# Which weight chunks are streamed in a recurrent attention kernel, and where the last tokens' output projection runs

## The chip, the cores and the metric

One core of one Trainium2 chip. The metric is the device time of one execution in microseconds (us), lower is better.

## The reference

The program computes two independent things and joins them: a long convolution (part A, the first 0.3 ms, not touched by the change) and attention over 64 segments of 32 tokens with 8 memory tokens (part B). The output at the memory tokens of one segment is the memory of the next, so part B is a chain of 64 segments. Cut to part B:

```python
# D = 1024, 32 heads of 128; seg_len 32, M = 8 memory tokens, n_seg = 64
for s in range(n_seg):
    h = concat([mem, x[:, s*32:(s+1)*32]], axis=1)          # 40 rows
    q, k, v = h @ Wq, h @ Wk, h @ Wv                        # three 1024 x 4096 weights, bf16
    p = softmax(mask(q @ k.T * scale))
    o = (p @ v) @ Wo                                        # 4096 x 1024
    mem = o[:, :M]                                          # needed by the next segment
    outs.append(o[:, M:])
```

The four weights are 32 MB; the kernel keeps part of them on the chip and reads the rest again in every segment.

## The kernel before

The weights are cut into 64 chunks of 512 KB: 8 each for K, Q, V in two head groups (48), and 16 for Wo. 43 chunks stay resident (`Wearly`, `Wlate`); 21 are streamed in every segment through a ring of six buffers, chosen evenly over the 64:

```python
NSTREAM = 21; RING = 6
order = [...K0, Q0, K1, Q1, V0, V1 (8 chunks each), then Wo (16)...]
for i in range(64):
    if ((i + 1) * NSTREAM) // 64 > (i * NSTREAM) // 64:
        streamed.add(order[i])
# [cut]
def fetch():                       # next chunk of the endless list of streamed chunks
    t = ring.tile([128, 2048], BF, tag="wring", name="wring")
    nc.sync.dma_start(t[:], stream_src(uses[n]))
def done(ch):                      # a streamed chunk was used: its buffer is refilled
    if ch in streamed:
        used[0] += 1
        fetch()
```

The last eight of a segment's 32 input tokens are called last tokens; their output does not feed the recurrence, so it can wait. Their attention output is gathered in `OTB` over four consecutive segments, and every fourth segment (`j == NB - 1`, below "the fourth") multiplies each Wo chunk twice: once for its own other 32 rows (24 tokens and the 8 memory rows), and once for the 32 rows of `OTB`. The four matmuls that use one chunk in a projection are called a group below: the "last V group" is the end of a segment's projections. That four column groups work side by side shows in the timeline of the kernel before: four matmuls of 256 columns, of 0.28 us each, start 0.107 us after the four before them.

```python
def load_x(s):                     # 192 KB: input rows and ready-made K/Q parts of segment s
    rec = one.tile([128, 768], BF, tag="rec", name="rec")     # one buffer
    nc.gpsimd.dma_start(rec[:], REC[:, s, :])
# [cut] fill_mem: PE transposes Y, VectorE copies the memory rows into rec (line 614)

def out_proj(hps, OT):
    for hp in hps:
        w = weight((3, hp, 0))
        for hh in range(2):
            lhs = [(OT[:, c, i, :], 0)]
            if j == NB - 1:
                lhs.append((OTB[:, c, 4 * g + i, :], 256))
            for src, o in lhs:
                for dq in range(4):          # four column groups of the array, side by side
                    nc.tensor.matmul(yacc[32 * dq:32 * dq + 32, o:o + 256], lhsT=src,
                                     rhs=w[:, hh * 1024 + dq * 256:hh * 1024 + (dq + 1) * 256], ...)
        done(ch)

# one segment, cut to its order on PE
k0 = Proj(0, 0).run().evac(); q0 = Proj(1, 0).run().evac()    # Proj: 8 chunks, 4 matmuls each
k1 = ...; q1 = ...; scores(0); pv0 = Proj(2, 0)...; scores(1)
pv1 = Proj(2, 1).run(4); attend(0); pv1.run(4)
if s + 1 < n_seg:
    load_x(s + 1)                  # waits until the last V matmul has read rec
out_proj(range(0, 5), OT0); attend(1); out_proj(range(5, 8), OT0); out_proj(range(8, 16), OT1)
nc.scalar.copy(Y[:], yacc[:, 0:256])
fill_mem(pend[s + 1][0], Y)        # then the next segment's K projection can start
```

Of the kernel before, what the change touches and what calls it, by code (L numbers as in the profile page):

```python
# [9 lines left out]
BF = mybir.dt.bfloat16  # L10
F32 = mybir.dt.float32
# [10 lines left out]
NSTREAM = 21  # L22
# [370 lines left out]
def b_kernel(ctx: ExitStack, tc, x, mem0, Wq, Wk, Wv, Wo, outb, n_seg):  # L393
    nc = tc.nc
    SEG = 32
    NX = 24
    NB = 4
# [14 lines left out]
    for hp in range(16):  # L412
        order.append((3, hp, 0))
    streamed = set()
    for i in range(64):
        if ((i + 1) * NSTREAM) // 64 > (i * NSTREAM) // 64:
            streamed.add(order[i])
    resident = [ch for ch in order if ch not in streamed]
    early = resident[:NEARLY]
# [3 lines left out]
    ring_order = [ch for ch in order if ch in streamed]  # L423

    def dram_chunk(ch):
        m, a, g = ch
        return Wo_v[a] if m == 3 else W_v[m][a, g]

    def dst_view(ap, ch):
        return ap.rearrange("p (hh d) -> p hh d", hh=2) if ch[0] == 3 else ap  # L430

    def stream_src(ch):
        return WS[ring_order.index(ch), :, 0:2048]
# [3 lines left out]
    REC = dram.tile([128, n_seg, 768], BF, name="REC")  # L437
    VBD = dram.tile([n_seg, 8, 4, 4, 256], BF, name="VBD")
    WS = dram.tile([len(ring_order), 128, PITCH], BF, name="WS")
    for ch in ring_order:  # L440
        if ch[0] == 3:
            nc.gpsimd.dma_start(dst_view(stream_src(ch), ch), dram_chunk(ch))

    const = ctx.enter_context(tc.tile_pool(name="b_const", bufs=1))
    ident = const.tile([128, 128], BF, name="ident")
    make_identity(nc, ident[:])
# [4 lines left out]
    res = {}  # L451
# [38 lines left out]
    with ExitStack() as c0:  # L490
# [42 lines left out]
        for m in (0, 1):  # L533
            for g in range(2):
                ws = group(m, g)
                stage = st.tile([128, n_seg, 16, 8], BF, tag="stage", name="stage")
                for hl in range(16):
                    ps = ps0.tile([128, 512], F32, tag="ps0", name="kb_ps")
                    for kc in range(8):
                        nc.tensor.matmul(ps[:], lhsT=ws[kc][:, hl * 128:(hl + 1) * 128],  # L540
                                         rhs=XBT[:, kc].rearrange("p s t -> p (s t)"),
                                         start=(kc == 0), stop=(kc == 7))
                    evac(stage[:, :, hl, :], ps[:].rearrange("p (s t) -> p s t", t=8))
                o = 256 * (m + 1) + 128 * g
                nc.sync.dma_start(REC[:, :, o:o + 128], stage[:].rearrange("p s h t -> p s (h t)"))
        for g in range(2):
            ws = group(2, g)
            for tb in range(4):
                vst = st.tile([128, 4, 512], BF, tag="vst", name="vst")
                for c in range(4):  # L550
                    ps = ps0.tile([128, 512], F32, tag="ps0", name="vb_ps")
                    for kc in range(8):
                        nc.tensor.matmul(ps[:], lhsT=XBT[:, kc, 16 * tb:16 * tb + 16, :].rearrange("p s t -> p (s t)"),  # L553
                                         rhs=ws[kc][:, c * 512:(c + 1) * 512], start=(kc == 0), stop=(kc == 7))
# [13 lines left out]
    one = ctx.enter_context(tc.tile_pool(name="b_one", bufs=1))  # L568
    two = ctx.enter_context(tc.tile_pool(name="b_two", bufs=2))
    ps_acc = ctx.enter_context(tc.tile_pool(name="b_ps_acc", bufs=2, space=PSUM))  # L570
# [8 lines left out]
    def fetch():  # L579
        n = len(loaded)  # L580
        if n < len(uses):
            t = ring.tile([128, 2048], BF, tag="wring", name="wring")
            nc.sync.dma_start(t[:], stream_src(uses[n]))
            loaded.append(t)

    def weight(ch):
        if ch in res:
            return res[ch]
        assert uses[used[0]] == ch
        return loaded[used[0]]  # L590

    def done(ch):
        if ch in streamed:
            loaded[used[0]] = None
            used[0] += 1
            fetch()
# [21 lines left out]
    with tc.manual_schedule():  # L618
# [6 lines left out]
            nc.scalar.dma_start(Y0[32 * dq + NX:32 * dq + SEG, :], mem0[:, dq * 256:(dq + 1) * 256])  # L625
        fill_mem(pend[0][0], Y0)

        OTB = None
        for s in range(n_seg):
            b, j = s // NB, s % NB  # L630
            hT, KBs, QBs = pend.pop(s)
# [16 lines left out]
            class Proj:  # L648


                def __init__(self, m, g):
                    self.m, self.g, self.kc = m, g, 0
                    self.acc = ps_acc.tile([128, 512], F32, tag="acc", name="acc")

                def run(self, n=8):
                    for kc in range(self.kc, self.kc + n):
                        ch = (self.m, kc, self.g)
                        w = weight(ch)
                        for c in range(4):
                            nc.tensor.matmul(self.acc[32 * c:32 * c + 32, :], lhsT=hT[:, kc, :],  # L660
                                             rhs=w[:, c * 512:(c + 1) * 512],
                                             start=(kc == 0), stop=(kc == 7), tile_position=(0, 32 * c))
                        done(ch)
                    self.kc += n
                    return self
# [30 lines left out]
            def softmax_b(S):  # L696
                ssum = two.tile([128, 5], F32, tag="ssum", name="ssum")
                nc.vector.tensor_reduce(out=ssum[:], in_=S, op=ALU.add, axis=AX.X)
                nc.vector.reciprocal(ssum[:], ssum[:])
                nc.vector.tensor_tensor(out=P_pad[:, :, 0:32], in0=S[:, :, 0:32],  # L700
                                        in1=ssum[:].unsqueeze(2).to_broadcast([128, 5, 32]), op=ALU.mult)
                own = P_pad[:].rearrange("p b k -> p (b k)")[:, 32:320].rearrange("p (i w) -> p i w", w=72)
                nc.vector.tensor_tensor(out=own[:, 0:4, 0:8], in0=S[:, 0:4, 32:40],
                                        in1=ssum[:, 0:4].unsqueeze(2).to_broadcast([128, 4, 8]), op=ALU.mult)
                nc.vector.scalar_tensor_tensor(
                    out=P_pad[:, 4, 32:64].rearrange("p (i t) -> p i t", i=4),
                    in0=S[:, 4:5, 32:40].to_broadcast([128, 4, 8]), scalar=ssum[:, 4:5],
                    in1=rowhead[:].unsqueeze(2).to_broadcast([128, 4, 8]), op0=ALU.mult, op1=ALU.mult)
                PT = one.tile([128, 2, 4, 40], BF, tag="PT", name="PT")
                for kb in range(2):  # L710
                    ks = slice(32 * kb, 32 * kb + 32)
                    nc.vector.transpose(out=PT[:, kb, :, 0:32], in_=P_pad[:, 0:4, ks])
                    nc.vector.transpose(out=PT[:, kb, :, 32:40], in_=P_pad[:, 4, ks])
                return PT
# [14 lines left out]
            def o_view(g):  # L729
                return OTp[:, :, 160 * g:160 * g + 160].rearrange("p c (i q) -> p c i q", i=4)  # L730

            def evac_o(g):
                OT = one.tile([128, 4, 4, 32], BF, tag="rotA" if g else "rotB", name="OT")
                nc.scalar.copy(OT[:], o_view(g)[:, :, :, 0:32])  # L734
                return OT

            def evac_ob(g):
                nc.vector.tensor_copy(OTB[:, :, 4 * g:4 * g + 4, 8 * j:8 * j + 8], o_view(g)[:, :, :, 32:40])  # L738

            def out_proj(hps, OT):  # L740
                for hp in hps:
                    ch = (3, hp, 0)
                    w = weight(ch)
                    for hh in range(2):
                        h = 2 * hp + hh
                        g, c, i = h // 16, (h % 16) // 4, h % 4
                        lhs = [(OT[:, c, i, :], 0)]
                        if j == NB - 1:
                            lhs.append((OTB[:, c, 4 * g + i, :], 256))
                        for src, o in lhs:  # L750
                            for dq in range(4):
                                nc.tensor.matmul(yacc[32 * dq:32 * dq + 32, o:o + 256], lhsT=src,  # L752
                                                 rhs=w[:, hh * 1024 + dq * 256:hh * 1024 + (dq + 1) * 256],
                                                 start=(h == 0 and o == 0), stop=(h == 31 and o == 0),
                                                 skip_group_check=(o > 0), tile_position=(0, 32 * dq))
                    done(ch)

            if j == 0:
                OTB = one.tile([128, 4, 8, 32], BF, tag="OTB", name="OTB")
            Sp = ps_s.tile([128, 2, 5, 40], F32, tag="S", name="S")  # L760
            OTp = ps_o.tile([128, 4, 512], F32, tag="OTp", name="OTp")
            k0 = Proj(0, 0).run().evac()
            q0 = Proj(1, 0).run().evac()
            KT0 = keys(0)
            last_queries(0)
# [19 lines left out]
            pv1 = Proj(2, 1).run(4)  # L785
            attend(0, PT0, V0, OTp)
            OT0 = evac_o(0)
            PT1 = softmax_b(Sp[:, 1])
            evac_ob(0)
            pv1.run(4)  # L790
# [3 lines left out]
            yacc = ps_acc.tile([128, 512], F32, tag="acc", name="yacc")  # L794
            out_proj(range(0, 5), OT0)
            attend(1, PT1, V1, OTp)
            OT1 = evac_o(1)
            evac_ob(1)
            out_proj(range(5, 8), OT0)
            out_proj(range(8, 16), OT1)  # L800
            Y = one.tile([128, 256], BF, tag="Y", name="Y")
            nc.scalar.copy(Y[:], yacc[:, 0:256])  # L802
            if s + 1 < n_seg:
                fill_mem(pend[s + 1][0], Y)
            nc.gpsimd.dma_start(bass.AP(outb.tensor, outb.offset + SEG * s * 2048, [[256, 4], [2048, 32], [1, 256]]), Y[:])  # L805
            if j == NB - 1:
                YB = one.tile([128, 256], BF, tag="OTB", name="YB")
                nc.vector.tensor_copy(YB[:], yacc[:, 256:512])
                for dq in range(4):
                    nc.gpsimd.dma_start(  # L810
                        bass.AP(outb.tensor, outb.offset + (SEG * NB * b + NX) * 2048 + 256 * dq,
                                [[2048 * SEG, NB], [2048, 8], [1, 256]]), YB[32 * dq:32 * dq + 32, :])


@with_exitstack
# [65 lines left out]
```

## Time and profile before

| | us |
|---|---|
| median of the first three runs | 2481.6 (2478.2 to 2485.7) |
| span of the profiled execution | 2487.5 |
| part A, preparation and start of B, up to the first segment's Y | 602.7 |
| ordinary segment (three of four) | 28.6 |
| the fourth segment | 33.1 |

Starts of the ScalarE copies of `Y`, each of which ends a segment (timeline of ScalarE, kernel before; start, duration, instruction, idle time before it):

```profile
1367.89 0.37 ACT L802 CAST Y<-yacc 128x256 bf16<-128x256 f32 x1 [3.33 <-PE yacc L752]
...
1400.97 0.37 ACT L802 CAST Y<-yacc 128x256 bf16<-128x256 f32 x1 [6.61 <-PE yacc L752]
...
1429.90 0.37 ACT L802 CAST Y<-yacc 128x256 bf16<-128x256 f32 x1 [4.55 <-PE yacc L752]
...
1457.74 0.37 ACT L802 CAST Y<-yacc 128x256 bf16<-128x256 f32 x1 [3.88 <-PE yacc L752]
```

The first difference, 33.1 us, is a fourth segment, the next two, 28.9 and 27.8, are ordinary ones. Windows of the kernel before, over the end of that fourth segment and then of an ordinary one:

```profile
core 0: us, PE busy (x) PEld busy (x) DVE busy (x) ACT busy (x) POOL busy (x), PEclk, DMA share, GB/s
...
1392.00:1396.00 4.00, 2.70 (x117) 2.62 (x120) 0.29 (x1) 0.58 (x1) 0.00 (x0) 1.00 1.04 399
1396.00:1400.00 4.00, 1.88 (x71) 1.60 (x63) 0.00 (x0) 0.00 (x0) 0.00 (x0) 1.00 0.84 308
1400.00:1404.00 4.00, 3.20 (x75) 1.77 (x70) 0.53 (x2) 0.37 (x1) 0.72 (x1) 1.00 0.70 225
1404.00:1408.00 4.00, 3.18 (x56) 1.38 (x49) 0.42 (x1) 1.17 (x2) 0.01 (x1) 1.00 0.94 284
...
1424.00:1428.00 4.00, 2.62 (x100) 1.70 (x92) 0.29 (x1) 0.58 (x1) 0.00 (x0) 1.00 1.03 400
1428.00:1432.00 4.00, 2.75 (x54) 1.43 (x57) 0.19 (x1) 0.37 (x1) 1.44 (x3) 1.00 1.03 411
```

The last column is the point: around the Y of the ordinary segment (1429.90) the DMA engines never slow down; around the Y of the fourth (1400.97) they fall to 225 GB/s for want of requests (between 1388.14 and 1400.96 the ring's issues lie 1.3 to 3.7 us apart, and a chunk takes 1.28 us).

The chain of waits before that same Y (start, length, what; "issue" is time in which PE waited for nothing that the profile shows):

```profile
1391.84 1.46 issue
...
1396.58 2.12 issue
```

The output projection of this fourth segment stood still twice, and not for the ring. (The prediction's 1.6 and 2.4 us are the same two stops, counted from the start of one matmul to the start of the next.) Such stops are called fetch waits below, after the queue that the page calls "instruction": they end 1.2 to 1.6 us after one of its packets has ended.

### The profile page before, as it was taken

Reading aid. Unit: us, or ns where it says so; the run is one execution under the profiler, and the core shown is the slowest. Engines: PE = TensorE matmul, PEld = TensorE weight load, DVE = VectorE, ACT = ScalarE, POOL = GpSimd, SP = SyncE. Lnnn points to the kernel's source line nnn. Section 1 sums busy time; section 2 is a strip of 40 time slices with the busy share of each in tenths; the row PEclk is TensorE's granted clock in tenths of the full one; section 3 lists DMA queues with packets and bytes.
Section 4 is the critical chain, followed back from the end, with each engine's and each line's share of the span. In section 5 each row is a group of like instructions: output and inputs, shape, how many; then the busy total and the mean of one; then the engine's idle time right before and its main releaser. Section 6 shows DMA issues by size and latency. Waiting matters only on the chain.

```text
span 2487.5 us, 76464 instructions
## 1 busy us (share of the span) xinstructions
PE 1782.3 (72%) x33598; PEld 886.9 (36%) x33620; DVE 674.8 (27%) x2203; ACT 639.9 (26%) x1143; POOL 365.5 (15%) x1019
## 2 busy tenths in 40 slices
PE   3555279845777777777777777777777777777776
PEld 1221044322343333433343334343434343343433
DVE  5977222111222222222222222222222222222222
ACT  6965011101222222222222222222222222222221
POOL 5034000000111101111111111111111111111011
PEclk8888679878999999999999999999999999999999
DMA  8886965579999999999999999999999999999997
GB/s 286 309 280 216 361 225 143 174 249 393 399 374 393 387 379 396 373 400 376 401 377 398 372 399 360 394 368 402 360 398 374 400 366 400 368 386 385 373 389 288
DMA packets 317559, 875.09 MB, mean 352 GB/s; under 512 B 84684, under 2 KB 92908, under 8 KB 317223
## 3 DMA queue, kind: packets, MB, share of 16 engines
q1 hardware_dynamic: 287064, 800.75, 84.7%
q0 software_dynamic: 20048, 45.76, 5.3%
q10 hardware_dynamic: 10112, 23.68, 2.8%
q8 instruction: 263, 4.31, 0.7%
q14 instruction: 72, 0.59, 0.1%
HBM read 810.69 MB, written 62.39 MB: 351 GB/s over the span
## 4 chain that ended last, share of the span: by engine, by line
DMA 53%; PE 31%; issue 5%; DVE 3%; POOL 1%; ACT 1%; SPq 0%; DVEq 0%; POOLq 0%; ACTq 0%
DMA wring<-WS 47%; PE acc L660 12%; PE yacc L752 7%; PE kb_ps L540 4%; PE vb_ps L553 2%; PE qk_tp L675 1%; DMA pw<-in_B_Wv_dram 1%; DMA Wearly<-in_B_Wk_dram 1%; DMA zt<-SZ 1%; POOL Yre L342 1%; DMA Wlate<-in_B_Wv_dram 1%; DMA X_sb<-in_B_x_dram 1%; PE S L683 1%; PE S L679 1%; ACT Y L802 0%
## 5 line engine op out<-in xcount | busy, mean ns | idle before, releaser
L660 PEld LDWEIGHTS <-rec 128*32 128x32 bf16 x12288 | 326.7, 98 | 640.2 <-issue 422.0
L660 PE MATMUL acc<-wring,rec 128*32 128x512 bf16 x3840 | 394.8, 398 | 201.1 <-DMA wring<-WS 190.7
L669 ACT CAST qkv_sb<-acc 128x512 bf16<-128x512 f32 x384 | 224.7, 585 | 843.3 <-PE acc L660 796.5
L660 PE MATMUL acc<-Wearly,rec 128*32 128x512 bf16 x4608 | 378.1, 404 | 21.6 <-DVE rec L614 21.6
L660 PE MATMUL acc<-Wlate,rec 128*32 128x512 bf16 x3840 | 331.7, 386 | 0.2 <-issue 0.2
L752 PEld LDWEIGHTS <-OT 128*32 128x32 bf16 x8192 | 239.3, 99 | 247.9 <-issue 183.3
L752 PE MATMUL yacc<-Wlate,OT 128*32 128x256 bf16 x5120 | 261.4, 283 | 30.2 <-issue 29.8
L752 PE MATMUL yacc<-wring,OT 128*32 128x256 bf16 x3072 | 183.9, 284 | 127.9 <-DMA wring<-WS 111.6
L637 POOL COPY KT<-rec 128x128 bf16<-128x128 bf16 x128 | 38.7, 302 | 657.1 <-PE S L686 591.3
L805 POOL DMA_DIRECT2D out_dram<-Y x64 | 46.2, 721 | 565.1 <-ACT Y L802 556.2
L766 DVE COPY KT<-qk_tp 128x512 bf16<-128x512 bf16 x64 | 27.2, 425 | 359.2 <-PE qk_tp L675 359.2
L614 DVE COPY rec<-y_tp 128x64 bf16<-128x64 bf16 x64 | 12.3, 192 | 405.4 <-PE y_tp L613 405.4
L734 ACT CAST OT<-OTp 128x512 bf16<-128x512 f32 x128 | 74.9, 585 | 183.6 <-PE OTp L725 179.9
L691 DVE TENSOR_REDUCE mx<-S 128x5 f32<-128x200 f32 x128 | 47.2, 368 | 244.1 <-PE S L686 238.2
L802 ACT CAST Y<-yacc 128x256 bf16<-128x256 f32 x64 | 23.8, 372 | 340.6 <-PE yacc L752 340.6
L675 PE MATMUL qk_tp<-ident,qkv_sb 128*128 128x128 bf16 x1024 | 102.8, 224 | 0.0
L752 PE MATMUL yacc<-Wlate,OTB 128*32 128x256 bf16 x1280 | 91.1, 291 | 15.7 <-issue 15.7
L607 POOL DMA_DIRECT2D rec<-REC x64 | 37.0, 578 | 403.9 <-issue 272.6
L752 PEld LDWEIGHTS <-OTB 128*32 128x32 bf16 x2048 | 82.0, 103 | 29.1 <-issue 23.0
L738 DVE CAST OTB<-OTp 128x128 bf16<-128x128 f32 x128 | 34.7, 271 | 206.9 <-ACT OT L734 206.9
L675 PEld LDWEIGHTS <-qkv_sb 128*128 128x128 bf16 x1024 | 58.5, 98 | 77.1 <-issue 62.8
L540 PE MATMUL kb_ps<-XBT,Wearly 128*128 128x512 bf16 x281 | 83.0, 384 | 1.7 <-ACT XBT L507 1.2
(197 smaller groups left out, 2163.6 us busy)
## 6 DMA issues: line engine op xcount, KB each, us to landing
wring<-WS SPq DMA_DIRECT2D x1344, 512.0 KB, 7.5
rec<-REC POOLq DMA_DIRECT2D x64, 192.0 KB, 6.3
SK<-s_sb SPq DMA_DIRECT2D x16, 512.0 KB, 4.6
SU<-s_sb SPq DMA_DIRECT2D x16, 512.0 KB, 3.4
Kg<-SK ACTq DMA_DIRECT2D x32, 256.0 KB, 5.0
Ug<-SU SPq DMA_DIRECT2D x32, 256.0 KB, 5.1
REC<-stage SPq DMA_DIRECT2D x4, 2048.0 KB, 13.2
pw<-in_B_Wv_dram SPq DMA_DIRECT2D x16, 512.0 KB, 8.2
```

The source lines that it names most:

```text
L540: nc.tensor.matmul(ps[:], lhsT=ws[kc][:, hl * 128:(hl + 1) * 128], rhs=XBT[:, kc].rearrange("p s t -> p (s t)"), start=(kc == 0), stop=(kc ...
L553: nc.tensor.matmul(ps[:], lhsT=XBT[:, kc, 16 * tb:16 * tb + 16, :].rearrange("p s t -> p (s t)"), rhs=ws[kc][:, c * 512:(c + 1) * 512], st ...
L607: nc.gpsimd.dma_start(rec[:], REC[:, s, :])
L637: nc.gpsimd.tensor_copy(KT[:, :, :, 32:40], KBs[:, 128 * g:128 * g + 128].rearrange("p (c i t) -> p i c t", c=4, i=4))
L660: nc.tensor.matmul(self.acc[32 * c:32 * c + 32, :], lhsT=hT[:, kc, :], rhs=w[:, c * 512:(c + 1) * 512], start=(kc == 0), stop=(kc == 7), t ...
L669: nc.scalar.copy(sb[:], self.acc[:])
L675: nc.tensor.transpose(tp[:, i * 128:(i + 1) * 128], sb[:, i * 128:(i + 1) * 128], ident[:])
L691: nc.vector.tensor_reduce(out=mx[:], in_=S, op=ALU.max, axis=AX.X)
L734: nc.scalar.copy(OT[:], o_view(g)[:, :, :, 0:32])
L738: nc.vector.tensor_copy(OTB[:, :, 4 * g:4 * g + 4, 8 * j:8 * j + 8], o_view(g)[:, :, :, 32:40])
L752: nc.tensor.matmul(yacc[32 * dq:32 * dq + 32, o:o + 256], lhsT=src, rhs=w[:, hh * 1024 + dq * 256:hh * 1024 + (dq + 1) * 256], start=(h == ...
L805: nc.gpsimd.dma_start(bass.AP(outb.tensor, outb.offset + SEG * s * 2048, [[256, 4], [2048, 32], [1, 256]]), Y[:])
```

## The change

Its intent: keep every Wo chunk resident, so that the output projection never waits for the ring, and take the doubled work out of the fourth output projection: it runs in a `Tail` after Y and between the first eight K chunks of the next segment. Sizes, number of streamed chunks and ring stay the same. The core of the diff, cuts marked:

```diff
-    for i in range(64):
-        if ((i + 1) * NSTREAM) // 64 > (i * NSTREAM) // 64:
+    for i in range(48):
+        if ((i + 1) * NSTREAM) // 48 > (i * NSTREAM) // 48:
             streamed.add(order[i])
# [cut] the copies of streamed Wo chunks to WS fall away
+        class Tail:
+            def __init__(self, OTB, b):
+                self.OTB, self.b, self.h = OTB, b, 0
+                self.acc = ps_acc.tile([128, 512], F32, tag="acc", name="tail_acc")
+            def run(self, n):       # the next n heads: 4 matmuls each, resident weights
# [cut]
# [cut] out_proj loses the OTB part and done(ch)
-            k0 = Proj(0, 0).run().evac()
+            k0 = Proj(0, 0)
+            for _ in range(8):
+                k0.run(1)
+                if tail is not None:
+                    tail.run(3)
+            k0 = k0.evac()
# [cut]
             nc.scalar.copy(Y[:], yacc[:, 0:256])
+            if j == NB - 1:
+                tail = Tail(OTB, b)
+                tail.run(6)
             if s + 1 < n_seg:
                 fill_mem(pend[s + 1][0], Y)
# [cut] output DMA
+            if tail is not None:
+                tail.run(4 if s + 1 < n_seg else 32)
```

More of the change, by code (lines that the diff above doesn't have):

```diff
@@ L439, in b_kernel @@
     WS = dram.tile([len(ring_order), 128, PITCH], BF, name="WS")
-    for ch in ring_order:
-        if ch[0] == 3:
-            nc.gpsimd.dma_start(dst_view(stream_src(ch), ch), dram_chunk(ch))
     const = ctx.enter_context(tc.tile_pool(name="b_const", bufs=1))
@@ L626, in b_kernel, with store @@
         fill_mem(pend[0][0], Y0)
-        OTB = None
+        class Tail:
[3 more added lines that the diff above has]
+            def run(self, n):
+                for h in range(self.h, min(self.h + n, 32)):
+                    w = res[(3, h // 2, 0)]
+                    g, c, i = h // 16, (h % 16) // 4, h % 4
+                    for dq in range(4):
+                        o = (h % 2) * 1024 + dq * 256
+                        nc.tensor.matmul(self.acc[32 * dq:32 * dq + 32, 0:256], lhsT=self.OTB[:, c, 4 * g + i, :],
+                                         rhs=w[:, o:o + 256], start=(h == 0), stop=(h == 31),
+                                         tile_position=(0, 32 * dq))
+                    if h == 31:
+                        self.store()
+                self.h = min(self.h + n, 32)
+            def store(self):
+                YB = one.tile([128, 256], BF, tag="OTB", name="YB")
+                nc.vector.tensor_copy(YB[:], self.acc[:, 0:256])
+                for dq in range(4):
+                    nc.gpsimd.dma_start(
+                        bass.AP(outb.tensor, outb.offset + (SEG * NB * self.b + NX) * 2048 + 256 * dq,
+                                [[2048 * SEG, NB], [2048, 8], [1, 256]]), YB[32 * dq:32 * dq + 32, :])
+        OTB = tail = None
         for s in range(n_seg):
@@ L746, in out_proj @@
                         g, c, i = h // 16, (h % 16) // 4, h % 4
-                        lhs = [(OT[:, c, i, :], 0)]
-                        if j == NB - 1:
-                            lhs.append((OTB[:, c, 4 * g + i, :], 256))
-                        for src, o in lhs:
-                            for dq in range(4):
-                                nc.tensor.matmul(yacc[32 * dq:32 * dq + 32, o:o + 256], lhsT=src,
-                                                 rhs=w[:, hh * 1024 + dq * 256:hh * 1024 + (dq + 1) * 256],
-                                                 start=(h == 0 and o == 0), stop=(h == 31 and o == 0),
-                                                 skip_group_check=(o > 0), tile_position=(0, 32 * dq))
-                    done(ch)
-            if j == 0:
-                OTB = one.tile([128, 4, 8, 32], BF, tag="OTB", name="OTB")
+                        for dq in range(4):
+                            nc.tensor.matmul(yacc[32 * dq:32 * dq + 32, 0:256], lhsT=OT[:, c, i, :],
+                                             rhs=w[:, hh * 1024 + dq * 256:hh * 1024 + (dq + 1) * 256],
+                                             start=(h == 0), stop=(h == 31), tile_position=(0, 32 * dq))
             Sp = ps_s.tile([128, 2, 5, 40], F32, tag="S", name="S")
             OTp = ps_o.tile([128, 4, 512], F32, tag="OTp", name="OTp")
-            k0 = Proj(0, 0).run().evac()
+            k0 = Proj(0, 0)
[4 more added lines that the diff above has]
+            k0 = k0.evac()
+            tail = None
             q0 = Proj(1, 0).run().evac()
@@ L787, in b_kernel @@
             OT0 = evac_o(0)
+            if j == 0:
+                OTB = one.tile([128, 4, 8, 32], BF, tag="OTB", name="OTB")
             PT1 = softmax_b(Sp[:, 1])
@@ L805, in b_kernel @@
             nc.gpsimd.dma_start(bass.AP(outb.tensor, outb.offset + SEG * s * 2048, [[256, 4], [2048, 32], [1, 256]]), Y[:])
-            if j == NB - 1:
-                YB = one.tile([128, 256], BF, tag="OTB", name="YB")
-                nc.vector.tensor_copy(YB[:], yacc[:, 256:512])
-                for dq in range(4):
-                    nc.gpsimd.dma_start(
-                        bass.AP(outb.tensor, outb.offset + (SEG * NB * b + NX) * 2048 + 256 * dq,
-                                [[2048 * SEG, NB], [2048, 8], [1, 256]]), YB[32 * dq:32 * dq + 32, :])
+            if tail is not None:
+                tail.run(4 if s + 1 < n_seg else 32)
 @with_exitstack
```

## The prediction

> **What bounds the kernel now.** The first 574 us build the convolution and tables; then 64 segments run back to back. Between the ScalarE copies that end a segment (timeline of ScalarE) lie 28.6 us for the first three of each block of four and 33.1 us for the fourth. The chain that ended last is 47% "DMA wring<-WS". In windows inside a segment DMA share is 1.0 and about 408 GB/s; in the DMA records the ring's queue moves 410 GB/s, so a 512 KB chunk takes 1.28 us, and 21 chunks plus 0.33 MB of other traffic need about 27.7 us. Three of four segments are thus DMA bound. In the fourth the output projection is doubled: PE waits on "issue" twice (1.6 and 2.4 us in one segment), the ring drains, and the windows show 308, 225, 284, 345 GB/s before 400 comes back. That loses about 4.9 us.
>
> The "issue" gaps end about 1.4 us after a 16 KB packet on the instruction queue (263 packets, 4.31 MB, in the page's queue table), and lie 256 instructions apart. [...]
>
> **What the change does.** Still 21 chunks per segment and a ring of 6, so no byte less. All 21 now fall in the K, Q, V projections; the output projection streams none. 128 matmuls per block of four (0.107 us per four, 3.4 us) leave the fourth output projection and go between its end and the next K projection. Preparation loses six HBM-to-HBM copies and gains six writes.
>
> **The critical path.** Do six chunks in flight cover the time from the last V chunk's use to the first K chunk's? Without instruction waits I add from the timeline: ten heads 1.1, attention with its evacuation 1.4, 16 more heads 1.7, copy of Y, transposes and copy to the next input 1.45, two resident K chunks 0.4: about 6.0 us. In the saturated state a chunk's last data comes 5.4 us after issue, and PE gets it 2 us later; so at the last V use only about 5.5 us of data are still to come (6 with the record load). The next issue comes at 6.4 us, its data 1.0 to 1.6 us later; cold ring chunks at the start took 1.8, 1.5, 1.9 us, after a drained ring 2.6 and 2.7. So each ordinary segment loses an estimated 2 to 4 us of transfer: 28.6 becomes about 30.7. Dense output projections (256 instructions in 3.4 us, against about 5.5 us per fetched block under load) may add tenths.
>
> The fourth segment: its gap becomes 6.0 + 0.95 (tail heads before the first streamed chunk) + about 1.5 of fetch waits; estimate 33.5, about as before. The doubled work is moved, not hidden: it lies where the ring is full and idle.
>
> Sum: 48 x 2.1 + 16 x 0.4 = +107 us; preparation about -5. **Predicted 2585 us, range 2500 to 2660; faster 0.07, same 0.17, slower 0.76.**
>
> **What would show it.** Segments near 30.7 and 33.5. No wait of the output projection on the ring; longer waits of the projections on it. Mean rate in the steady part below 375 GB/s, with a dip in every segment around Y. "issue" waits in the output projection of all segments.
>
> **What would make it wrong.** If the gap stays under about 5 us, or the ring ramps up as at the cold start or better, ordinary segments stay at 28.6, and the fourth falls to 30 or less: then about 2440. If fetch waits strike each output projection by 1.5 us or more, it is 2650 or above.

The sum: +107 and -5 on 2484 is about 2585 us. What the traces show for its fetch terms is this: in the kernel before, where two stops fall into one fourth output projection, 256 instructions apart, their ends lie 5.1 to 6.2 us apart, median 5.7 (about the "5.5 us"), and the fourth ones lose 2.95 us each to such stops on average.

## More of the kernel before

The page of the kernel before (its slices are 62 us each; PEclk is the granted TensorE clock in tenths, GB/s what the DMA engines moved; the groups give busy time, mean ns, and idle time before them with its main releaser; PE is TensorE's matmuls, PEld its weight loads, DVE VectorE, ACT ScalarE, POOL GpSimd, SP SyncE):

```profile
...
PEclk8888679878999999999999999999999999999999
GB/s 286 309 280 216 361 225 143 174 249 393 399 374 393 387 379 396 373 400 376 401 377 398 372 399 360 394 368 402 360 398 374 400 366 400 368 386 385 373 389 288
...
q1 hardware_dynamic: 287064, 800.75, 84.7%
...
q8 instruction: 263, 4.31, 0.7%
...
DMA wring<-WS 47%; PE acc L660 12%; PE yacc L752 7%; PE kb_ps L540 4%; PE vb_ps L553 2%; PE qk_tp L675 1%; DMA pw<-in_B_Wv_dram 1%; DMA Wearly<-in_B_Wk_dram 1%; DMA zt<-SZ 1%; POOL Yre L342 1%; DMA Wlate<-in_B_Wv_dram 1%; DMA X_sb<-in_B_x_dram 1%; PE S L683 1%; PE S L679 1%; ACT Y L802 0%
...
L660 PE MATMUL acc<-wring,rec 128*32 128x512 bf16 x3840 | 394.8, 398 | 201.1 <-DMA wring<-WS 190.7
...
L752 PE MATMUL yacc<-wring,OT 128*32 128x256 bf16 x3072 | 183.9, 284 | 127.9 <-DMA wring<-WS 111.6
...
L614 DVE COPY rec<-y_tp 128x64 bf16<-128x64 bf16 x64 | 12.3, 192 | 405.4 <-PE y_tp L613 405.4
...
wring<-WS SPq DMA_DIRECT2D x1344, 512.0 KB, 7.5
rec<-REC POOLq DMA_DIRECT2D x64, 192.0 KB, 6.3
```

The chain that ended last is 47% reading of the ring. The output projection waits for the ring (111.6 us), and the copy into `rec` waits for PE, never for the load of `rec`, though that load takes 6.3 us from issue to landing.

## The result, and the profile after

| | before | after |
|---|---|---|
| median, us | 2483.6 (4 runs) | 2683.9 (4 runs, 2679.1 to 2688.1) |
| ratio to before, 95% interval | 1 | 1.081 (1.078 to 1.084) |
| ordinary segment, us | 28.6 | 32.4 |
| segment with the doubled work or the tail, us | 33.1 | 35.0 |
| up to the first Y, us | 602.7 | 594.4 |

Ratios are the mean time of one kernel's fast runs over that of the other's in the same rounds, so not quite the ratio of the medians. Segment lengths are means over the trace, from one segment's last V group on PE to the next one's.

The sum closes: over the 63 intervals the changed kernel is 48 x 3.8 + 15 x 1.9 = 211 us longer; up to the last V group of the first segment it is 5.8 us shorter and after that of the last segment 6.3, which leaves the 199 us between the two spans. The change is slower, as predicted, but by 8.1% and not by 4%: the time lies outside the predicted range.

The page of the changed kernel, the lines that answer to those above:

```profile
...
PEclk8897599878988899998889999888889889989889
...
GB/s 243 305 285 249 362 171 185 221 373 359 335 339 345 358 336 346 344 356 337 350 328 347 343 361 352 355 331 348 342 348 336 346 332 365 344 343 341 342 349 280
...
q1 hardware_dynamic: 287448, 800.75, 78.5%
...
DMA wring<-WS 40%; DMA rec<-REC 11%; PE acc L684 10%; PE kb_ps L536 4%; PE yacc L772 3%; PE tail_acc L637 2%; PE vb_ps L549 2%; DMA X_sb<-in_B_x_dram 1%; PE qk_tp L699 1%; POOL Yre L342 1%; DMA Wlate<-in_B_Wo_dram 1%; DMA pw<-in_B_Wv_dram 1%; DMA out_dram<-ot 1%; PE S L707 1%; PE S L703 1%
...
L684 PE MATMUL acc<-wring,rec 128*32 128x512 bf16 x5376 | 597.2, 429 | 422.8 <-DMA wring<-WS 419.6
...
L772 PE MATMUL yacc<-Wlate,OT 128*32 128x256 bf16 x8192 | 279.1, 283 | 36.6 <-issue 35.5
...
L610 DVE COPY rec<-y_tp 128x64 bf16<-128x64 bf16 x64 | 12.3, 192 | 313.9 <-DMA rec<-REC 213.5
...
wring<-WS SPq DMA_DIRECT2D x1344, 512.0 KB, 7.2
rec<-REC POOLq DMA_DIRECT2D x64, 192.0 KB, 6.3
```

The same 800.75 MB go through the ring's queue, at about 345 GB/s in the steady slices where it was about 385. The output projection no longer waits for the ring, and the projections wait for it twice as long as before (419.6 us; before 190.7). (Before, the output projection's 111.6 us come on top of that.) New is the wait for the record: `rec<-REC` makes up 11% of the chain, and the copy into `rec` now waits for that load (213.5 us). It still takes 6.3 us; what shrank is the time it could hide in.

The starts of Y in the changed kernel (the second interval, 30.2 us, and the third, 34.1, are ordinary; the first, 35.4, carries a tail):

```profile
1489.48 0.37 ACT L826 CAST Y<-yacc 128x256 bf16<-128x256 f32 x1 [2.96 <-PE yacc L772]
...
1524.85 0.37 ACT L826 CAST Y<-yacc 128x256 bf16<-128x256 f32 x1 [3.14 <-PE yacc L772]
...
1555.08 0.37 ACT L826 CAST Y<-yacc 128x256 bf16<-128x256 f32 x1 [2.04 <-PE yacc L772]
...
1589.17 0.37 ACT L826 CAST Y<-yacc 128x256 bf16<-128x256 f32 x1 [3.12 <-PE yacc L772]
```

Windows of the changed kernel around the Y at 1524.85, with the columns explained above:

```profile
1514.00:1518.00 4.00, 2.44 (x64) 1.00 (x63) 2.73 (x12) 1.00 (x3) 0.00 (x0) 0.99 1.01 402
1518.00:1522.00 4.00, 4.00 (x108) 2.80 (x110) 0.25 (x1) 1.17 (x2) 0.59 (x1) 0.58 1.03 406
1522.00:1526.00 4.00, 2.38 (x70) 1.55 (x66) 0.23 (x2) 0.37 (x1) 0.48 (x1) 1.00 0.62 241
1526.00:1530.00 4.00, 3.33 (x60) 1.51 (x59) 0.00 (x0) 0.58 (x1) 1.64 (x7) 1.00 0.61 163
1530.00:1534.00 4.00, 1.60 (x24) 0.76 (x24) 0.42 (x1) 0.58 (x1) 0.00 (x0) 1.00 0.94 312
```

This is an ordinary segment, and it shows the dip that only the fourth had before: 241, 163, 312 GB/s. In the window from 1518 the granted clock is 0.58: the output projection began at half clock.

The chain of waits of the changed kernel in order of time (start, length, what), from the last V group of that segment on, and then at the same place one segment later:

```profile
1511.03 6.83 DMA wring<-WS
1517.90 0.62 PE acc L684 x4
1518.52 2.13 PE yacc L772 x40
...
1523.38 0.81 issue
1524.19 0.64 PE yacc L772 x15
1524.85 0.38 ACT Y L826
...
1525.90 1.31 PE acc L684 x21
1527.21 6.42 DMA wring<-WS
...
1550.30 0.42 PE acc L684 x4
...
1551.28 7.00 DMA rec<-REC
...
1558.65 1.70 PE acc L684 x13
```

Two different gaps. At 1517.90 the output projection was slow (ten heads in 2.1 us, and an "issue" wait of 0.81), so the record was in time. After the V group at 1550.30 the output projection was quicker (Y starts 4.8 us later, against 6.9), and PE then waited for the record until 1558.65. In both the first streamed K group came more than 8 us after the last V group.

**What a segment loses, counted from the DMA records.** I add up, over a segment, how far the rate of ring and record traffic lies under 410 GB/s, the rate in the saturated stretches; what is left of a segment is 27.6 to 27.8 us in each row. That remainder is only its bytes at this rate, the same in every kernel here, so the table says where in a segment the time is lost, and not yet why. "Gap" is the time from the start of the last V group to the start of the first streamed K group; the chunk that frees goes out about 0.45 us later.

| segment | length | gap | lost until that issue | lost in the next 8 us | rest |
|---|---|---|---|---|---|
| before, ordinary | 28.6 | 10.4 | 0.2 | 0.6 | 0.1 |
| before, fourth | 33.1 | 15.1 | 3.2 | 1.8 | 0.4 |
| after, ordinary | 32.4 | 8.3 | 2.3 | 2.4 | 0.1 |
| after, with tail | 35.0 | 9.8 | 3.9 | 3.0 | 0.3 |

Before, the gap is longer but contains six streamed Wo chunks, each of which sends a request. After, the gap contains none. In it the ring moves 2.36 MB, 5.8 us at 410 GB/s, and is then empty.

### The profile page after: what moved, and what is told of

Same layout as the page of the kernel before. It is cut to its first block, busy times and chain, and to the rows that moved or that the text cites. A ratio compares the mean times of both kernels' runs of the same rounds, so it can differ in the third digit from the quotient of the medians.

```text
span 2686.3 us, 76444 instructions
## 1 busy us (share of the span) xinstructions
PE 1859.6 (69%) x33620; PEld 904.0 (34%) x33620; DVE 679.5 (25%) x2203; ACT 639.4 (24%) x1143; POOL 365.1 (14%) x1019
## 3 DMA queue, kind: packets, MB, share of 16 engines
q1 hardware_dynamic: 287448, 800.75, 78.5%
q8 instruction: 263, 4.31, 0.6%
## 4 chain that ended last, share of the span: by engine, by line
DMA 57%; PE 24%; issue 10%; DVE 2%; POOL 1%; ACT 1%; SPq 0%; DVEq 0%; POOLq 0%; ACTq 0%
DMA wring<-WS 40%; DMA rec<-REC 11%; PE acc L684 10%; PE kb_ps L536 4%; PE yacc L772 3%; PE tail_acc L637 2%; PE vb_ps L549 2%; DMA X_sb<-in_B_x_dram 1%; PE qk_tp L699 1%; POOL Yre L342 1%; DMA Wlate<-in_B_Wo_dram 1%; DMA pw<-in_B_Wv_dram 1%; DMA out_dram<-ot 1%; PE S L707 1%; PE S L703 1%
## 5 line engine op out<-in xcount | busy, mean ns | idle before, releaser
L684 PE MATMUL acc<-wring,rec 128*32 128x512 bf16 x5376 | 597.2, 429 | 422.8 <-DMA wring<-WS 419.6
L684 PE MATMUL acc<-Wearly,rec 128*32 128x512 bf16 x4608 | 493.5, 436 | 85.6 <-DVE rec L610 75.3
L772 PE MATMUL yacc<-Wlate,OT 128*32 128x256 bf16 x8192 | 279.1, 283 | 36.6 <-issue 35.5
L772 PEld LDWEIGHTS <-OT 128*32 128x32 bf16 x8192 | 219.2, 100 | 75.1 <-issue 46.9
L684 PE MATMUL acc<-Wlate,rec 128*32 128x512 bf16 x2304 | 238.8, 419 | 0.0
L791 DVE COPY QT<-qk_tp 128x512 bf16<-128x512 bf16 x64 | 27.2, 424 | 306.3 <-PE qk_tp L699 306.3
L637 PE MATMUL tail_acc<-Wlate,OTB 128*32 128x256 bf16 x2048 | 94.0, 289 | 10.8 <-issue 10.8
L536 PE MATMUL kb_ps<-XBT,Wearly 128*128 128x512 bf16 x288 | 99.8, 383 | 1.2 <-ACT XBT L503 1.2
L610 DVE COPY rec<-y_tp 128x64 bf16<-128x64 bf16 x64 | 12.3, 192 | 313.9 <-DMA rec<-REC 213.5
L762 DVE CAST OTB<-OTp 128x128 bf16<-128x128 f32 x128 | 35.4, 276 | 221.7 <-ACT OT L758 221.6
L536 PE MATMUL kb_ps<-XBT,pw 128*128 128x512 bf16 x224 | 85.7, 382 | 0.0
L668 POOL COPY QBm<-rec 128x32 bf16<-128x32 bf16 x512 | 84.0, 210 | 0.0
```

Source lines behind the costliest of these rows:

```text
L536: nc.tensor.matmul(ps[:], lhsT=ws[kc][:, hl * 128:(hl + 1) * 128], rhs=XBT[:, kc].rearrange("p s t -> p (s t)"), start=(kc == 0), stop=(kc ...
L637: nc.tensor.matmul(self.acc[32 * dq:32 * dq + 32, 0:256], lhsT=self.OTB[:, c, 4 * g + i, :], rhs=w[:, o:o + 256], start=(h == 0), stop=(h ...
L668: nc.gpsimd.tensor_copy(q[:, :, 40 * i:40 * i + 8], QBs[:, 128 * g:128 * g + 128].rearrange("p (c i t) -> p c i t", c=4, i=4)[:, :, i, :])
L684: nc.tensor.matmul(self.acc[32 * c:32 * c + 32, :], lhsT=hT[:, kc, :], rhs=w[:, c * 512:(c + 1) * 512], start=(kc == 0), stop=(kc == 7), t ...
L772: nc.tensor.matmul(yacc[32 * dq:32 * dq + 32, 0:256], lhsT=OT[:, c, i, :], rhs=w[:, hh * 1024 + dq * 256:hh * 1024 + (dq + 1) * 256], star ...
```

## The experiments

The theory ("gap"): a segment is as long as its transfers (27.7 us) plus the time in which too few chunks are asked for; that is set by the gap against what six buffers hold, plus a slow restart. The gap came out 2.3 us longer than predicted, by the wait for the record, the "issue" waits and the half clock. Rivals: the half clock of TensorE (409 us of it in part B after, 146 before, from the clock records); the moved projection itself.

### Loading the record early (a_rec), and its control (b_rec)

The input half of the record gets its own double-buffered tile and is asked for a segment ahead (Y takes the place of another small tile to make room). The other half, read only by GpSimd, is then free early and comes early too. Both kernels give correct results.

```diff
-        rec = one.tile([128, 768], BF, tag="rec", name="rec")
-        nc.gpsimd.dma_start(rec[:], REC[:, s, :])
+        kq = one.tile([128, 512], BF, tag="kq", name="kq")
+        nc.gpsimd.dma_start(kq[:], REC[:, s, 256:768])
+    def load_h(s):
+        t = two.tile([128, 256], BF, tag="hT", name="hT")
+        nc.gpsimd.dma_start(t[:], REC[:, s, 0:256])
 # [cut] load_h(s + 1) at the start of segment s
-            Y = one.tile([128, 256], BF, tag="Y", name="Y")
+            Y = one.tile([128, 256], BF, tag="PT", name="Y")
```

> The changed kernel with the input half of the segment record in a tile of its own, double buffered and loaded a segment ahead, so that the copy of the memory rows into it no longer waits for that load. Gap theory with the record load as the missing term: the wait from Y to the first K matmul falls from 2.3 to about 1.1 us, the gap from the last V group to the first streamed K group from 8.6 to about 7.3, segments get 1.2 us shorter, 2600 to 2620 us in all. Rival, half clock of TensorE: the load is hidden behind a clock that was slow anyway, time stays within 15 us of 2684.

> Control: the same edit in the kernel before. There the output projection waits for the ring and the record is in time (Y to K 1.06 us), so both theories expect no change, within 10 us of 2484.

Measured: a_rec 2666.0 us (ratio to before 1.072, 95% 1.069 to 1.076), only 18 us less than the changed kernel. Its page has the copy of the memory rows waiting for PE again, not for a load:

```profile
L617 DVE COPY hT<-y_tp 128x64 bf16<-128x64 bf16 x64 | 12.3, 192 | 241.5 <-PE y_tp L616 241.5
```

The gap fell as expected, in ordinary segments from 8.3 to 7.1 us, but the segments only from 32.4 to 31.9. (The traced executions differ by 31 us, 2686 and 2656; the medians by the 18.) By time alone this is as near to the rival's "within 15 us" as to the theory; the gap is what tells them apart. The DMA records say where the rest went. Between the last V group and the first new issue the ring moved 2.36 MB in the changed kernel and 2.34 in a_rec; but the other traffic in that time fell from 0.26 to 0.01 MB. The record load had been filling 0.6 us of an otherwise empty gap, and has to be moved in saturated time now. So the wait for the record is a real part of the gap, and taking it away is worth at most half its length (0.5 of 1.1 us by the traces, 18 / 64 = 0.3 us by the medians). My expectation counted only the wait. The control came out at 2492.7 us, 0.4% slower than before (1.000 to 1.007): nothing to gain there, as expected.

### The streaming alone (b_s48)

```diff
-    for i in range(64):
-        if ((i + 1) * NSTREAM) // 64 > (i * NSTREAM) // 64:
+    for i in range(48):
+        if ((i + 1) * NSTREAM) // 48 > (i * NSTREAM) // 48:
```

This is the kernel before with this edit alone; the result is correct.

> Half of the change: the kernel before with all 21 streamed chunks in K, Q, V, but the last tokens' projection still inside the fourth output projection. Gap theory: ordinary segments as in the changed kernel (32.4 us); the fourth has about 4 us more of output projection in the gap and takes 36 to 37 us; in all 2700 to 2730 us, so streaming alone explains the loss and the moved projection gives some of it back. Rival, the moved projection is what costs (it is interleaved with the K projection): ordinary segments near 29 and the whole below 2560.

Measured: 2729.3 us (1.099, 1.095 to 1.103); ordinary segments 32.4 us, the fourth 37.4 with a gap of 12.5 us, of which 6.8 us of transfer were lost before the next issue. The streaming alone costs 246 us. The moved projection gives back 45 us of it (2729 to 2684), and is not what costs.

### One ring buffer less (a_ring5)

The changed kernel with `RING = 5`. A deeper ring was not run: the depth was varied downwards only.

> The changed kernel with five ring buffers in place of six [...]. Gap theory: one chunk less in flight is 1.28 us less cover in every gap, so each segment loses about 1.3 us, 2684 + 80 = 2750 to 2780. Rival, half clock or instruction fetch on PE as the cause: the ring depth matters little, under 2710.

Measured: 2769.3 us (1.115, 1.111 to 1.118), 85 us more than the changed kernel, where 64 x 1.28 = 82 were expected. The rivals inside PE expected under 2710, so the depth of the ring does count. That the number was met so well is partly luck, though: ordinary segments grew by 1.3 us (32.4 to 33.7), those with the tail by 0.8, and of the 1.3 only 0.6 were lost between the last V group and the next issue (2.4 to 3.0 us, in a gap that was itself 0.4 us shorter); the other 0.7 were lost more than 8 us after the restart (0.1 to 0.8 us), where the theory expected no loss.

### Half the output projection left out (a_rec_half, b_half)

Wrong results: every second head is left out of the output projection, in a_rec and in the kernel before (there both products of that head, while all chunks are still streamed).

```diff
-                    for hh in range(2):
+                    for hh in range(1):
```

> Wrong result on purpose: the changed kernel with the early record load, and half the heads of the ordinary output projection left out (128 instructions and 1.7 us of matmuls less, between the last V group and Y). Gap theory: that time lies open, segments lose as much as the gap shrinks, about 2 us with its fetch waits: 2540 to 2560. If a segment of the changed kernel were bound by transfer or by something outside the gap: less than 40 us below 2666.

> Wrong result on purpose: the same heads left out of the kernel before, every weight still streamed. Gap theory: ordinary segments are bound by transfer and stay at 28.3 to 28.8 us, although as much PE work is gone; only the fourth gets short, 29 us in place of 33: about 2415. If PE work of the output projection counts in ordinary segments too: below 2370.

Measured: a_rec_half 2540.8 us, 125 below a_rec: the gap shrinks by 2.0 us (7.1 to 5.2), ordinary segments by 1.7 (31.9 to 30.2). b_half 2423.7 us: ordinary segments stay at 28.6, and the fourth falls from 33.1 to 29.0. The same matmuls lie open in the changed kernel and behind the transfer in the kernel before. Even at 5.2 us the changed segments lose 2.6 us, 1.9 of it in the 8 us of the restart. So shortening the gap to about 5 us does not bring back the 28.6 us that the prediction names as the outcome of a gap under about 5.

### Keeping TensorE warm (a_rec_warm)

```diff
                         done(ch)
+                        if (self.m, self.g) == (2, 1):
+                            if kc == 0:
+                                self.fill = ps_t.tile([128, 512], F32, tag="tp", name="fill")
+                            for f in range(1 + kc % 2):
+                                nc.tensor.matmul(self.fill[:], lhsT=ident[:], rhs=res[(3, 0, 0)][:, 512 * f:512 * f + 512],
+                                                 start=True, stop=True)
```

The products are never read; the result is correct. In the clock records of the changed kernel (last section) PE was busy for 11 to 60% in the windows of 3.41 us that half clock followed, so a busier PE might keep the full clock.

> The changed kernel with the early record load, with 12 idle 128x512 matmuls per segment put in the V projection's ring waits to keep TensorE busy, so that it does not enter the output projection at half clock. Half clock as a main cause: 40 us or more below 2666. Gap theory with the half clock as a small part (0.38 us lost per us at half clock, 0.9 us of it per gap): 10 to 25 us below 2666; if the filler itself delays the chunks, no gain.

The 0.38 us per us is what a least-squares fit over the 48 ordinary segments of the changed kernel gives, of the time from the last V group to Y against the half clock and the "issue" waits in it.

Measured: 2715.0 us (1.092, 1.088 to 1.096), 49 us slower than a_rec. It did what it was built for: in the trace no output projection began at half clock (0.0 us of it between last V group and Y, 0.85 in a_rec), and the ordinary gap fell from 7.1 to 6.8 us. But the segments grew from 31.9 to 32.6: between last V group and the next issue the ring moved 1.94 MB in place of 2.34. The likely reason, argued and not shown, is that the filler made PE free the V chunks later, so that fewer were asked for when the gap began; and two of its twelve products stand after the last V chunk, inside the gap itself. No branch of the expectation had a loss. So this run does not rule out the half clock by its time. What does is where the half clock lies: of 6.6 us of it in an ordinary segment of the changed kernel 0.95 is in the gap of 8.3 us, which at full clock would be an estimated 0.5 us shorter (half of 0.95), and 4.0 lie more than 8 us after the restart, where only 0.1 us of transfer is lost. The 1.6 us of it in the restart are not tested.

### Moving only part of the work (b_hyb, b_hyb2)

Trying to beat both: the kernel before, but in the fourth segment only the 12 last-token heads with streamed weights stay; the other 20 run between the next K chunks, three after each (b_hyb), or four after each from the fourth chunk on (b_hyb2).

```diff
-                        if j == NB - 1:
+                        if j == NB - 1 and ch in streamed:
                             lhs.append((OTB[:, c, 4 * g + i, :], 256))
 # [cut] the changed kernel's Tail over the resident heads, adding into yacc[:, 256:512]
+                if tail is not None:                       # b_hyb2: and k0.kc > 3
+                    tail.run(3)                            # b_hyb2: 4
```

> A version meant to beat both: the streaming of the kernel before, spread over all 64 chunks, and in every fourth segment only the last-token heads whose output weights are streamed stay in place (12 of 32); the 20 heads with resident weights run among the next segment's K projection. Gap theory: the ring never goes unread for longer than in an ordinary segment plus about 1.3 us, so the fourth segment falls from 33.1 to 29 or 30 us and the rest stay: 2484 - 16 x 3.5 = about 2425, range 2405 to 2450. Rival, moving the last tokens' heads costs as much as it saves: within 15 us of 2484.

> The hybrid again, with the 20 moved heads only after the fourth K chunk, so that the first streamed chunk of the segment is released as early as in the kernel before. If the hybrid failed because the heads stood ahead of that chunk: the transfer lost behind it falls and the fourth segment comes from 32.1 to about 30.5 us, 2450 us in all. If the loss only moves to the following chunks: 2465 or more.

Measured: b_hyb 2473.8 us (0.995, 0.992 to 0.997), b_hyb2 2467.0 us (0.991, 0.989 to 0.993), both correct. The fourth segment came to 32.1 and 31.4 us, not to 29 or 30. In b_hyb 1.4 us of transfer were lost before the first issue of the next segment and 2.5 in the 8 us after it; in b_hyb2 1.1 and 2.1. The expectation for b_hyb was wrong: the loss moved from the output projection into the K projection, where the heads delay the freeing of chunks (from the first K matmul to the first streamed group 2.3 us, in ordinary segments 0.9). Putting them behind the first streamed chunk brought this back to 0.9 but helped only a little: 2467 us lies in the branch "the loss only moves to the following chunks". Both kernels are within 2% of the kernel before.

### Fewer instructions for the same products (b_wide)

The kernel before, but in the fourth segment each head is multiplied by four matmuls of 512 columns, two for its own tokens and two for `OTB`, in the four column groups side by side, in place of eight of 256 columns. The matmul time should be the same: in the kernel before four matmuls of 512 columns follow one another every 0.22 us on PE (K projection, 1402.67 to 1402.89), four of 256 every 0.11. The instructions (each matmul has its weight load: 33598 and 33620 on the page) fall from 16 to 8 for a head.

```diff
+                        if j == NB - 1:
+                            for q in range(4):
+                                src = OT[:, c, i, :] if q < 2 else OTB[:, c, 4 * g + i, :]
+                                o = hh * 1024 + (q % 2) * 512
+                                nc.tensor.matmul(yacc[32 * q:32 * q + 32, :], lhsT=src, rhs=w[:, o:o + 512],
+                                                 start=(h == 0), stop=(h == 31), tile_position=(0, 32 * q))
+                            continue
 # [cut] Y and the last tokens now lie as [64, 512]: four transposes and other output views
```

> A version meant to beat both: the kernel before, where every fourth output projection multiplies each head's weights by both left sides at once, 4 matmuls of 512 columns in place of 8 of 256. The matmul time is the same (four column groups side by side), the instructions of that stretch halve, 512 to 256. If the fourth segment is long because PE waits for instructions: it falls from 33.1 to 29 to 30 us, the gaps in PE before Y in that segment shrink from 4.3 us to the 3.7 us of ring waits seen in the others, and the whole is 2420 to 2440 us. If it is long because of the matmul time itself: 32 us or more, within 15 us of 2486.

Measured: 2432.5 us (0.977, 95% 0.976 to 0.979), correct, and faster than both. The fourth segment takes 29.0 us; 1.4 us of transfer are lost in it where it was 5.4. Gaps over 0.5 us in PE between the last V group and Y fall, counted as in the expectation from the start of one matmul to the start of the next, from 4.5 us to 1.2, below the 3.7 that I expected; as idle time of PE they fall from 3.5 us to 0.5, 3.0 and 0.04 of it on "issue" (PE is busy 4.00 and 3.68 of 4 us below). Windows of b_wide around the end of a fourth segment (its Y starts at 1384.27):

```profile
1376.00:1380.00 4.00, 4.00 (x94) 1.77 (x87) 0.29 (x1) 0.59 (x1) 0.00 (x0) 1.00 1.02 401
1380.00:1384.00 4.00, 3.68 (x72) 1.75 (x60) 0.00 (x0) 0.00 (x0) 0.00 (x0) 1.00 1.03 405
1384.00:1388.00 4.00, 2.98 (x58) 1.51 (x53) 0.89 (x2) 0.74 (x2) 0.70 (x1) 1.00 1.04 393
```

The dip to 308 and 225 GB/s of the kernel before is gone. So the fourth segment was long because PE waited for instructions, with the same matmuls to do. The trace of the kernel before says the same: all 48 "issue" gaps over 0.5 us in its output projections lie a multiple of 256 PE instructions apart, and end 1.2 to 1.6 us after a packet of the instruction queue has ended. The place that the change aimed at could be mended where it was.

## Why the prediction was wrong

**What held.** The bound (ordinary segments saturated at 410 GB/s, the fourth not), the mechanism (no request during the output projection, the ring runs empty in every segment), the direction, no wait of the output projection on the ring, the rate under 375 GB/s, preparation a little shorter (-8 us, predicted -5).

**The step that failed** is the sum for the gap: "about 6.0 us" from the last V use to the first streamed K chunk, and with it "28.6 becomes about 30.7". The gap measured 8.3 us in ordinary segments and the segments 32.4. Two terms of that sum were too small: the way from Y to the K matmuls, and the output projection up to Y. In ordinary segments:

- From Y to the K matmuls I took 1.05 us (within the 1.45 of the prediction), the value before. It measured 2.2: the copy into `rec` waited for the record load. That load is issued 1.0 us after the start of the last V group and took another 6.5 us to the copy on average; before, 8.3 us went by in that time anyway, so it was hidden by 2 us. The prediction shortened the stretch that hid it and did not ask what else ran there. Half or more of this term was given back, since the load's bytes moved in the gap (a_rec).
- From the last V group to Y I took 4.6 us. Segments without any wait took 4.57; the mean was 5.6. "Issue" gaps over 0.5 us in PE, such as the 0.81 at 1523.38, make 0.55 of the difference. They are fetch waits like those before: all 33 of them in the trace lie a multiple of 256 PE instructions apart (to within two records), and end 1.3 to 1.6 us after a packet of the instruction queue; 22 of the 48 ordinary output projections have one. The half clock makes an estimated 0.35 (half of the 0.7 us that it lasts there: a projection's four matmuls follow one another every 0.43 us at half clock, 1559.29 to 1559.72, and every 0.22 at full, 1562.51 to 1562.73). The prediction named the fetch waits as possible "tenths" and left them out of the sum, and did not think of the clock. What the two cost in ordinary segments is read from the trace, not tested by a run of its own.
- Two resident K chunks: 0.5 us, predicted 0.4.

At a gap of 6.0 the predicted 30.7 is about right: in a_rec, whose gaps vary, 8 of the 48 ordinary segments had no wait in it and a gap of 6.01 us, and they took 30.8 us on average (29.8 to 31.7). So the sum had its known terms right and lacked the waits. The forgotten load is the smaller part of the miss: without it (a_rec) the kernel was 18 us faster, and 81 us stay above the predicted 2585. What the ring still holds at the start of the gap was well estimated (predicted 6 us of data with the record, measured 2.36 + 0.26 MB = 6.4 us). The restart costs 2.4 us.

**The segment with the tail** was predicted at 33.5 and took 35.0; "about as before" was too good by 1.9 us. Its gap was predicted at 6.0 + 0.95 + 1.5 = 8.45 us and measured 9.8. The heads before the first streamed chunk cost 1.4 us and not 0.95: from Y to the first streamed group it took 4.2 us, in ordinary segments 2.7.

**In all** 48 x 1.7 + 16 x 1.5 = 106 us, about the 99 us between the predicted 2585 and the measured 2684. The range was too narrow: it held fetch waits of 1.5 us as the worst case and no forgotten wait.

The prediction's "PE gets it 2 us later" holds too: where PE waited for a chunk, it started on it 2.0 us (median) after the chunk's last data packet in the kernel before, and 1.4 us in the changed one. So part of what the six buffers have asked for has always moved already when PE gets to it, and only some 5.8 us of transfer are still to come.

## What to carry to other kernels

What counted here, where a stream at 410 GB/s was the bound, was that requests do not stop: a stretch with no consumer emptied the ring (2.3 us lost per ordinary segment) and then cost a restart too (2.4 us). So spread the streamed pieces over the whole period, above all over the stretch that waits for nothing else. When a stretch is made shorter, list every transfer that was issued before it and needed after it, with its time to landing (6.3 us for the record here): each is a new candidate for the wait. And before moving work away from a long stretch, ask whether it is long because of the work or because of its number of instructions; here half the instructions for the same products gained 2.3% (b_wide), where moving part of them gained 0.9% at most (b_hyb2).

## What else the traces show

- PE stood idle for 1.46 and 2.12 us at places 256 PE instructions apart in one fourth segment before, while the DMA engines moved 399 and 308 GB/s, and for 0.55 us on average in the ordinary output projections after. The trace of the kernel before has 263 packets of 16 KB, 4.31 MB in all, on the instruction queue. Halving the instructions of the fourth output projection of the kernel before took 2.3% off the whole (b_wide).
- Every stretch at half clock inside part B lasts 3.41 us or a multiple of it in the clock records, before and after, except the last one at the end of the program. Half clock came after stretches that were not idle: PE was busy for 54% of the 3.41 us before the half clock of 1517.92. Dividing the clock records of the changed kernel's part B into windows of 3.41 us gives, with the profile's busy times of PE: in the 97 windows at full clock that were followed by half clock PE was busy for 11 to 60% (median 41), in the 389 that were followed by full clock for 40 to 100%. In this trace full clock came back only after windows busy for 81% or more.
- The restart of the emptied queue is slow. After the gap of the changed kernel the first three 512 KB chunks took 2.1, 2.3 and 1.8 us each from first to last packet, against 1.4 in the saturated state (means over ordinary segments); the restart lost 2.4 us of transfer per segment. Requests alone do not explain it: the second and third chunk were asked for 0.6 and 1.4 us after the first, and their last packets came 5.0 and 6.4 us after it. Its cause stays open.
